# V of twelve blocks loaded as two halves of 64 partitions through two queues, in an attention kernel on one core

## The chip, the cores and the metric

The kernel runs on one core of one Trainium2 chip. The metric is device microseconds of one execution. Before the change the median of 3 runs is 631.32 us (631.2 to 632.54). Durations of single steps come from one profiled execution.

## The reference

Attention without a mask, for 8 x 16 = 128 heads, each with 16 queries, 2048 keys and head size 256, all in bf16:

```
scores = einsum('bhqd,bhkd->bhqk', q, k) * 256 ** -0.5
attn   = softmax(scores, axis=-1)
out    = einsum('bhqk,bhkd->bhqd', attn, v)
```

K and V have 134 MB each and are read once. The output has 1 MB.

## The kernel before, in words

**Blocks.** The 128 heads go in G = 16 blocks of 8 heads (8 heads by 16 queries are the 128 rows of a block's scores). One block needs K in two loads, e = 0 and 1 (below: K0 and K1), each of 128 partitions by T = 64 rows of 256 elements, 4 MiB; and V in one load of 128 partitions by 128 rows, 8 MiB, 64 KB into each partition. The tile `SL` has four slots of one K load each. Slots `VA` and `VB` together, seen as `VW`, hold V; slots `KA` and `KB` hold K0 and K1. There is one buffer for each, so K0 of the next block can come only when the QK matmuls have read the present K0, and V of the next block only when all PV matmuls of the present one are done.

**Queues.** All loads are issued by SyncE (SP), in one queue, in an order written out by hand (`on_sync`, L128). First q, then K of blocks 0 and 1, V of block 0 in two loads, K of block 2, V of block 1 in two loads (one for slot `VA`, one for slot `VB`, each of 128 partitions). Then a loop (L148) with j from 3 to 14: K0 of block j, K1 of block j, and `load_v(j - 1, 0, 2 * T)` (L152), the V load of block j - 1 in one piece: these are the twelve V loads of blocks 2 to 13. Then K of the last block in four loads, and V of blocks 14 and 15 in 3 and 9 pieces along the rows (`PIECES`, L104). Ahead of each load stands a wait for its slot: K for the counter `c_qk` (QK matmuls), V for `c_pv` (PV matmuls; it counts 8 for each block, one for 16 rows, and starts at 8). `load_v(w, 0, 128)` waits for `c_pv >= 8 * w + 8` (L131), and its DMA (L132) adds 16 to `s_v` when it has landed.

**TensorE (PE).** In round r of its loop (L340) it does the QK matmuls of block r (L296, L297), for r up to 13 also 20 spare matmuls into an unused bank (L356), then PV of block r - 1 (L317). Ahead of PV it waits for `c_ev` (the output bank has been evicted), `c_co[0]` (the first half of the weights is in place) and `s_v` (V has landed); in the middle of PV for `s_v0` and `c_co[1]`, the second half's weights.

**VectorE (DVE)** transposes K in place by 4-byte elements (L200: two instructions for K0, two for K1), takes the row maximum (L222), transposes the exponentials (L226, L227) and does part of the copies that set up PV's weights `PTz` (L207, L209).

**ScalarE (ACT)**, in block g (loop at L276): scaled copies of the next queries (L256), the exponential (L282), then `copies(0, (0, 1))` (L269) for the first half of the weights, which wait until PV of the block before is half done; then, for g other than 0, `evac(g + 1)` (L262): it waits for `c_pv >= 8 * (g + 1)`, that is for PV of the block before to end, and evicts its output; then eight copies for the second half. Ahead of its loop ACT adds 1 to each of three counters, `c_ev`, `c_ri` and `c_co[1]` (L271).

**GpSimd (POOL)** makes first increments of 11 semaphores (L168), among them 8 to `c_pv`, then sets buffers to zero and copies q. It has no work after the start.

Of the kernel before, what the change touches and what calls it, by code (L numbers as in the profile page):

```python
# [5 lines left out]
ALU = mybir.AluOpType  # L6
# [8 lines left out]
T = 64  # L15
# [5 lines left out]
def bass_standalone__softmax_full_bidir__sampling_kernel(  # L21
# [11 lines left out]
    last = G - 1  # L33
# [5 lines left out]
    vb = v.rearrange("b h s d -> (b h s) d").rearrange("(g p t) d -> g p t d", p=128, t=2 * T)  # L39
# [3 lines left out]
    with ExitStack() as es:  # L43
# [22 lines left out]
        def sem(name):  # L66
            return ec(nc.semaphore(name))
# [4 lines left out]
        s_kl = [sem("s_kla"), sem("s_klb")]  # L72
        s_v = sem("s_v")
        s_v0 = sem("s_v0")
        s_st = sem("s_st")
        c_pool = sem("c_pool")
        c_qt = sem("c_qt")
# [8 lines left out]
        c_ri = sem("c_ri")  # L86
        c_co = [sem("c_co0"), sem("c_co1")]
        c_mk = sem("c_mk")

        c_pv = sem("c_pv")  # L90
        c_ev = sem("c_ev")
# [16 lines left out]
        VW = SL[:, VA:VB + 1, :, :].rearrange("p a t d -> p (a t) d")  # L108
# [16 lines left out]
        def load_k(eng, g, e, slot, t0, n, s):  # L125
            eng.dma_start(SL[:, slot, t0:t0 + n, :], ku[2 * g + e, :, t0:t0 + n, :]).then_inc(s, 16)  # L126

        def on_sync(eng):  # L128
            def load_v(w, a, n):

                eng.wait_ge(c_pv, 8 * w + (a + n + C - 1) // C)  # L131
                eng.dma_start(VW[:, a:a + n, :], vb[w, :, a:a + n, :]).then_inc(s_p[a] if a else s_v, 16)  # L132

            eng.dma_start(QX, qh).then_inc(s_q, 16)
            for g, s0, s in ((0, VA, s_k0), (1, KA, s_k)):
                for e in range(2):
                    load_k(eng, g, e, s0 + e, 0, T, s[e])

            for e in range(2):
                eng.wait_ge(c_qk, 4 * e + 4)  # L140
                eng.dma_start(VW[:, T * e:T * e + T, :], vb[0, :, T * e:T * e + T, :]).then_inc(s_v0 if e else s_v, 16)
            for e in range(2):
                eng.wait_ge(c_qk, 4 * e + 12)
                load_k(eng, 2, e, KA + e, 0, T, s_k[e])
            for e in range(2):
                eng.wait_ge(c_pv, 4 * e + 12)
                eng.dma_start(VW[:, T * e:T * e + T, :], vb[1, :, T * e:T * e + T, :]).then_inc(s_v0 if e else s_v, 16)
            with nc.Fori(3, last, engines=[SP], hint_back_edge=True) as j:  # L148
                for e in range(2):
                    eng.wait_ge(c_qk, 8 * j + 4 * e - 4)  # L150
                    load_k(eng, j, e, KA + e, 0, T, s_k[e])
                load_v(j - 1, 0, 2 * T)  # L152
            for e in range(2):
                eng.wait_ge(c_qk, 8 * last + 4 * e - 4)
                load_k(eng, last, e, KA + e, 0, T // 2, s_k[e])
                load_k(eng, last, e, KA + e, T // 2, T // 2, s_kl[e])
            for w in PIECES:
                for a, n in PIECES[w]:
                    load_v(w, a, n)
            eng.wait_ge(c_ev, G)  # L160
            eng.dma_start(oh[:, 0:last, :], O_all[:, 2:G + 1, :]).then_inc(s_st, 16)
            eng.wait_ge(c_ev, G + 1)
            eng.dma_start(oh[:, last, :], O_all[:, G + 1, :]).then_inc(s_st, 16)
            eng.wait_ge(s_st, 32)

        def on_gpsimd(eng):

            for x, n in ([(c_pv, 8)] + [(x, 1) for x in s_kl] +  # L168
                         [(s_p[a], 16 * G - 16 * sum(a in dict(PIECES[w]) for w in PIECES)) for a in s_p]):
                eng.sem_inc(x, n)  # L170
            eng.memset(QW[:].rearrange("p e m x -> p (e m x)").bitcast(F32), 0.0).then_inc(c_qt, 1)
            zero = [PTz[:, e].rearrange("p t c -> p (t c)").bitcast(F32) for e in range(2)]
            eng.memset(zero[0], 0.0).then_inc(c_pool, 1)
            eng.memset(mk[:], 1.0).then_inc(c_mk, 1)
            eng.memset(P_sb[:, 0:16], 0.0).then_inc(c_mk, 1)
            eng.memset(P_sb[:, 2064:2080], 0.0).then_inc(c_mk, 1)
            eng.wait_ge(c_mk, 3)
            for r in range(4):
                eng.memset(mk[32 * r:32 * r + 16, :], 0.0).then_inc(c_mk, 1)
            eng.wait_ge(c_qt, 2)  # L180
            for n in range(16):

                eng.wait_ge(c_cq if n else c_pool, max(n, 1))
                eng.tensor_copy(*qx(n // 4, n % 4)).then_inc(c_cq, 1)  # L184

            eng.wait_ge(c_qw, 4)
            eng.wait_ge(c_cq, 16)
            eng.wait_ge(c_mk, 7)
            eng.memset(zero[1], 0.0).then_inc(c_pool, 1)
# [60 lines left out]
        def on_scalar(eng):  # L250
            def qwb(src):
                for a in range(4):
                    dv = QW[32 * a:32 * a + 32, :, 16 * a:16 * a + 64, :]
                    dv = bass.AP(tensor=dv.tensor, offset=QW[32 * a:32 * a + 32, 0, 16 * a, :].offset,
                                 ap=[list(dv.ap[0]), [1024 + 512, 2], [2, 64], [1, 2]])
                    eng.activation(dv, src(a), ACTF.Copy, scale=scale).then_inc(c_qw, 1)  # L256

            def evac(n):

                eng.wait_ge(c_pv, 8 * n)  # L260
                eng.wait_ge(c_ri, n)
                eng.activation(O_all[:, bass.ds(n, 1), :].rearrange("p o d -> p (o d)"), O_ps[:, 0:D], ACTF.Copy,  # L262
                               scale=rinv[:, bass.ds(n, 1)]).then_inc(c_ev, 1)

            def copies(e, rs):
                for r in rs:
                    for x in range(2):
                        dst, src, m = weights(e, r, x)
                        eng.activation(dst, src, ACTF.Copy, scale=m if x else 1.0).then_inc(c_co[e], 1)  # L269

            for x in (c_ev, c_ri, c_co[1]):  # L271
                eng.sem_inc(x, 1)
            eng.wait_ge(c_qt, 2)
            qwb(lambda a: QXu[0:32, a, 0:2, :, :])
            eng.wait_ge(c_pool, 2)
            with nc.Fori(0, G, engines=[ACT]) as g:  # L276
                eng.wait_ge(c_qk, 8 * g + 8)
                qwb(lambda a: QTu[32 * a:32 * a + 32, bass.ds(((g + 1) & 15) * 2, 2), :, :])
                eng.wait_ge(c_mx, g + 1)
                sv = S_ps[:, 0, :]  # L280
                sv = bass.AP(tensor=sv.tensor, offset=sv.offset, ap=[list(sv.ap[0]), [32, 64], [1, 2], [2, 16]])
                eng.activation(P_sb[:, 16:2064], sv, ACTF.Exp,  # L282
                               bias=negm[:], scale=1.0, accum_out=lsum[:]).then_inc(c_ex, 1)
                eng.wait_ge(c_pt, 2 * g + 2)
                eng.wait_ge(c_pv, 8 * g + 4)
                copies(0, (0, 1))
                gg = eng.to_reg(g)
                with eng.If_ne(gg, 0):
                    evac(g + 1)
                copies(1, (0, 1, 2, 3))  # L290

        def on_tensor(eng):
# [35 lines left out]
            with nc.Fori(0, 2, engines=[PE]) as e:  # L328
                for h in range(2):
                    with nc.Fori(0, 4, engines=[PE]) as b:  # L330
# [5 lines left out]
                        if h:  # L336
                            ins.then_inc(c_qk, 1)

            two = eng.alloc_register("two")
            with nc.Fori(1, G + 1, engines=[PE], hint_back_edge=True) as r:  # L340
                rr = eng.to_reg(r)
                r16 = eng.to_reg(16 * r)
                with eng.If_lt(rr, G):
                    for e in range(2):
                        for h in range(2):
                            eng.wait_ge(c_kt[e], 2 * r + h - 1)
                            if e + h == 0:
                                eng.wait_ge(c_ex, rr)
                            ins = qk(e, (2 * h, 2 * h + 1), KA + e)
                        ins.then_inc(c_qk, 4)  # L350

                    mid = eng.to_reg((r + 14) & 15)
                    with eng.If_lt(mid, 13):
                        with nc.Fori(0, SPARE, engines=[PE]) as x:
                            for _ in range(4):
                                mm(X_ps[:], QW[:, 1, :, 7], QT[:, 0:512], True, True, False)  # L356
                eng.wait_ge(c_ev, rr)
                eng.wait_ge(c_co[0], 8 * r)
                eng.wait_ge(s_v, r16)
                eng.reg_alu(two, r16, 32, ALU.min)  # L360
                pv(r16, two)

        on_sync(nc.sync)
        on_gpsimd(nc.gpsimd)
        on_vector(nc.vector)
        on_scalar(nc.scalar)
        on_tensor(nc.tensor)


# [26 lines left out]
```

## Time and profile before

| | |
|---|---|
| median of 3 runs | 631.32 us (631.2 to 632.54) |
| the profiled execution | 631.19 us, of which the span from first to last instruction 629.9 us |
| granted clock of TensorE | 0.978 |
| PE busy | 533.9 us (85%) |
| DVE busy | 419.4 us (67%) |
| ACT busy | 269.0 us (43%) |
| POOL busy | 26.0 us (4%) |
| moved by DMA | 270.54 MB, mean 430 GB/s |

The profile shows one execution. Busy time is an engine's own; instructions that wait or only issue a DMA don't count. The DMA engines have a row of their own. PE's matmuls are pipelined, so 85% busy does not mean that TensorE is at its peak. SPq is SyncE's sequencer, which issues the loads, and lines such as L317 are those of the code above. Where a row ends in brackets, they hold the engine's idle time ahead of it and what ended it.

### The profile page before, as it was taken

Reading aid. Unit: us, or ns where it says so; the run is one execution under the profiler, and the core shown is the slowest. Engines: PE = TensorE matmul, PEld = TensorE weight load, DVE = VectorE, ACT = ScalarE, POOL = GpSimd, SP = SyncE. Lnnn points to the kernel's source line nnn. Section 1 sums busy time; section 2 is a strip of 40 time slices with the busy share of each in tenths; the row PEclk is TensorE's granted clock in tenths of the full one; section 3 lists DMA queues with packets and bytes.
Section 4 is the critical chain, followed back from the end, with each engine's and each line's share of the span. In section 5 each row is a group of like instructions: output and inputs, shape, how many; then the busy total and the mean of one; then the engine's idle time right before and its main releaser. Section 6 shows DMA issues by size and latency. Waiting matters only on the chain.

```text
span 629.9 us, 7712 instructions
## 1 busy us (share of the span) xinstructions
PE 533.9 (85%) x3336; PEld 273.5 (43%) x2561; DVE 419.4 (67%) x193; ACT 269.0 (43%) x308; POOL 26.0 (4%) x30
## 2 busy tenths in 40 slices
PE   1657989889888897888988888988889888889997
PEld 0112734518244272532726336263362724518386
DVE  1989694865849657496574956749466594768740
ACT  1026562823437243362534525335263352732653
POOL 7800000000000000000000000000000000000000
PEclk9998999999898999989989999898999989999999
DMA  9999999999999999999999999999999999999999
GB/s 377 433 433 433 431 429 429 433 433 433 466 400 466 400 433 433 433 433 433 433 466 400 466 400 466 400 433 433 433 433 466 400 466 400 466 400 426 437 420 383
DMA packets 11152, 270.54 MB, mean 430 GB/s; under 512 B 1040, under 2 KB 3344, under 8 KB 3728
## 3 DMA queue, kind: packets, MB, share of 16 engines
q1 hardware_dynamic: 11152, 270.54, 100.0%
HBM read 269.48 MB, written 1.05 MB: 429 GB/s over the span
## 4 chain that ended last, share of the span: by engine, by line
DMA 57%; PE 33%; DVE 5%; issue 5%; SPq 0%; DVEq 0%; ACT 0%
DMA SL<-in_v_dram 51%; PE O_ps L317 31%; DMA SL<-in_k_dram 5%; DVE SL L200 3%; DVE PTb L227 1%; DVE negm L222 1%; PE X_ps L297 1%; PE S_ps L296 1%; PE S_ps L297 1%; DVE PTz L207 0%; DVE PTz L209 0%; SPq L132 0%; SPq L126 0%; ACT P_sb L282 0%; DVE O_all L247 0%
## 5 line engine op out<-in xcount | busy, mean ns | idle before, releaser
L200 DVE STREAM_TRANSPOSE SL<-SL 128x4096 f32<-128x4096 f32 (+1 forms) x63 | 280.6, 4492 | 88.0 <-DMA SL<-in_k_dram 87.6
L296 PE MATMUL S_ps<-SL,QW 128*128 128x512 bf16 (+1 forms) x512 | 205.1, 401 | 59.0 <-DVE SL L200 49.8
L317 PEld LDWEIGHTS O_ps<-SL,PTz 128*128 128x128 bf16 x2048 | 199.0, 98 | 113.9 <-issue 89.0
L317 PE MATMUL O_ps<-SL,PTz 128*128 128x256 bf16 x2048 | 226.4, 273 | 24.8 <-DMA SL<-in_v_dram 23.8
L297 PE MATMUL S_ps<-SL,QW 128*128 128x512 bf16 (+1 forms) x512 | 204.4, 399 | 0.0
L296 PEld LDWEIGHTS S_ps<-SL,QW 128*128 128x128 bf16 (+1 forms) x512 | 74.4, 145 | 230.1 <-issue 160.7
L256 ACT ACTIVATE QW<-QT 32x256 bf16 x64 | 26.8, 419 | 168.4 <-PE S_ps L297 167.2
L269 ACT ACTIVATE PTz<-PTa 16x1024 bf16<-16x1024 bf16 x32 | 33.8, 1056 | 128.9 <-PE O_ps L317 114.2
L222 DVE TENSOR_REDUCE negm<-S_ps 128x1 f32<-128x2048 f32 x16 | 36.6, 2289 | 58.3 <-PE S_ps L297 58.3
L269 ACT ACTIVATE PTz<-PTa,mk 32x1024 bf16<-32x1024 bf16 x64 | 72.3, 1130 | 0.0
L269 ACT ACTIVATE PTz<-PTb 16x1024 bf16<-16x1024 bf16 x64 | 67.2, 1051 | 1.2
L226 DVE STREAM_TRANSPOSE PTa<-P_sb 128x2048 bf16<-128x2048 bf16 x16 | 37.0, 2312 | 35.4 <-ACT P_sb L282 35.4
L297 PE MATMUL X_ps<-QT,QW 128*128 128x512 bf16 x260 | 58.2, 379 | 0.0
L227 DVE STREAM_TRANSPOSE PTb<-P_sb 128x2080 bf16<-128x2080 bf16 x16 | 36.8, 2302 | 0.0
L269 ACT ACTIVATE PTz<-PTb,mk 32x1024 bf16<-32x1024 bf16 x32 | 36.2, 1132 | 0.0
L282 ACT ACTIVATE P_sb<-S_ps,negm 128x2048 bf16<-128x2048 f32 x16 | 31.5, 1967 | 5.9 <-DVE negm L222 5.9
L262 ACT ACTIVATE O_all<-O_ps,rinv 128x256 f32 x15 | 7.1, 473 | 39.8 <-PE O_ps L317 39.8
L184 POOL COPY QT<-PTz 32x1024 bf16<-32x1024 bf16 x16 | 17.4, 1088 | 2.1 <-DVE PTz L194 1.2
L207 DVE TENSOR_SCALAR PTz<-PTb,mk 32x1024 bf16<-32x1024 bf16 x32 | 15.2, 476 | 0.0
L209 DVE COPY PTz<-PTa 16x1024 bf16<-16x1024 bf16 x32 | 13.5, 421 | 1.1
L247 DVE TENSOR_SCALAR O_all<-O_ps,rinv 128x256 bf16<-128x256 f32 x1 | 0.5, 483 | 20.2 <-PE O_ps L317 20.2
L296 PE MATMUL S_ps<-PTz 128*128 128x512 bf16 x1 | 0.6, 609 | 9.7 <-ACT QW L256 9.7
(18 smaller groups left out, 21.0 us busy)
## 6 DMA issues: line engine op xcount, KB each, us to landing
SL<-in_k_dram SPq DMA_DIRECT2D x30, 4096.0 KB, 24.1
SL<-in_v_dram SPq DMA_DIRECT2D x4, 4096.0 KB, 21.3
SL<-in_k_dram SPq DMA_DIRECT2D x4, 2048.0 KB, 22.3
SL<-in_v_dram SPq DMA_DIRECT2D x1, 3840.0 KB, 21.3
SL<-in_v_dram SPq DMA_DIRECT2D x1, 2496.0 KB, 22.0
SL<-in_v_dram SPq DMA_DIRECT2D x1, 2048.0 KB, 12.2
SL<-in_v_dram SPq DMA_DIRECT2D x1, 1856.0 KB, 24.7
SL<-in_v_dram SPq DMA_DIRECT2D x1, 1792.0 KB, 10.8
```

The source lines that it names most:

```text
L184: eng.tensor_copy(*qx(n // 4, n % 4)).then_inc(c_cq, 1)
L200: eng.transpose(x, x).then_inc(c_k0 if first else c_kt[e], n)
L207: ins = eng.tensor_scalar(out=dst, in0=src, scalar1=m, scalar2=None, op0=ALU.mult)
L222: eng.tensor_reduce(out=negm[:], in_=S_ps[:].rearrange("p c n -> p (c n)"), axis=AX.X, op=ALU.max, negate=True).then_inc(c_mx, 1)
L226: eng.transpose(fa[:, 0:2048], P_sb[:, 16:2064]).then_inc(c_pt, 1)
L227: eng.transpose(fb[:, 0:2080], P_sb[:, 0:2080]).then_inc(c_pt, 1)
L256: eng.activation(dv, src(a), ACTF.Copy, scale=scale).then_inc(c_qw, 1)
L269: eng.activation(dst, src, ACTF.Copy, scale=m if x else 1.0).then_inc(c_co[e], 1)
L282: eng.activation(P_sb[:, 16:2064], sv, ACTF.Exp, bias=negm[:], scale=1.0, accum_out=lsum[:]).then_inc(c_ex, 1)
L296: return eng.matmul(dst, w, x, start=start, stop=stop, skip_group_check=not check)
L297: return eng.add_instruction(mybir.InstMatmult(name=nc.get_next_instruction_name(), engine=PE, start_tensor_calc=start, stop_tensor_calc=stop,
L317: ins = eng.matmul(O_ps[:, 0:D], PTz[:, t // T, t % T, :], VW[:, t, :], start=(t == 0), stop=(t == 2 * T - 1))
```

## The change

The V loads of blocks 2 to 13 are each made as two loads of 64 partitions. SP issues the one for partitions 0 to 63 at the old place, with the old wait written out, and it adds 16 to `s_v`. ACT issues the one for partitions 64 to 127, with the same wait, between `copies(0, (0, 1))` and `evac(g + 1)`, for g from 2 to 13; it adds 16 to a new semaphore `s_v1`. PE waits for both ahead of PV: `s_v1` starts at 32, which stands for blocks 0 and 1, and the value waited for stops at 16 * last - 16 = 224, so that blocks 14 and 15 wait for nothing new. The increments of `c_ev`, `c_ri` and `c_co[1]` that ACT made at the start go to GpSimd's list, with the 32 of `s_v1`.

```diff
+        s_v1 = sem("s_v1")
...
 (on_sync, loop over j from 3 to 14)
-                load_v(j - 1, 0, 2 * T)
+                eng.wait_ge(c_pv, 8 * j)
+                eng.dma_start(VW[0:64, :, :], vb[j - 1, 0:64, :, :]).then_inc(s_v, 16)
...
 (on_gpsimd)
-            for x, n in ([(c_pv, 8)] + [(x, 1) for x in s_kl] +
+            for x, n in ([(c_pv, 8), (c_ev, 1), (c_ri, 1), (c_co[1], 1), (s_v1, 32)] + [(x, 1) for x in s_kl] +
...
 (on_scalar)
-            for x in (c_ev, c_ri, c_co[1]):
-                eng.sem_inc(x, 1)
...
                 with eng.If_ne(gg, 0):
+                    mid = eng.to_reg((g + 14) & 15)
+                    with eng.If_lt(mid, last - 3):
+                        eng.wait_ge(c_pv, 8 * g + 8)
+                        eng.dma_start(VW[64:128, :, :], vb[g, 64:128, :, :]).then_inc(s_v1, 16)
                     evac(g + 1)
...
 (on_tensor)
+            one = eng.alloc_register("one")
...
                 eng.wait_ge(s_v, r16)
+                eng.reg_alu(one, r16, 16 * last - 16, ALU.min)
+                eng.wait_ge(s_v1, one)
                 eng.reg_alu(two, r16, 32, ALU.min)
                 pv(r16, two)
```

## The prediction

> **What bounds the kernel now.** I read the page first, then the kernel's middle in one window, then the chain of waits, then single engines in one block. The page's slices of the span, its DMA queues and its chain by engine:
>
> ```profile
> span 629.9 us, 7712 instructions
> ...
> DMA  9999999999999999999999999999999999999999
> GB/s 377 433 433 433 431 429 429 433 433 433 466 400 466 400 433 433 433 433 433 433 466 400 466 400 466 400 433 433 433 433 466 400 466 400 466 400 426 437 420 383
> ...
> q1 hardware_dynamic: 11152, 270.54, 100.0%
> ...
> DMA 57%; PE 33%; DVE 5%; issue 5%; SPq 0%; DVEq 0%; ACT 0%
> ...
> SL<-in_k_dram SPq DMA_DIRECT2D x30, 4096.0 KB, 24.1
> ```
>
> One queue carries everything, its packets fill the sixteen DMA engines for the whole span, and the slices stand at 433 GB/s (466 and 400 alternate around it where a long row falls to one side). The kernel's middle in one window says it again (the last two columns are the DMA engines' share and GB/s):
>
> ```profile
> core 0: us, PE busy (x) PEld busy (x) DVE busy (x) ACT busy (x) POOL busy (x), PEclk, DMA share, GB/s
> 100.00:580.00 480.00, 422.65 (x2668) 215.94 (x2030) 325.52 (x154) 206.91 (x237) 0.00 (x0) 0.98 1.00 432
> ```
>
> At 433 GB/s a K load (4096 KB, 4.19 MB) takes 9.69 us, and V of one block (128 partitions of 64 KB by the code, 8.39 MB) takes 19.37 us. K0, K1 and V of a block together take 38.75 us. The chain of waits, in order of time, through one block:
>
> ```profile
> 233.51 24.23 DMA SL<-in_v_dram
> 257.75 0.23 issue
> 257.98 14.15 PE O_ps L317 x128
> 272.13 0.02 issue
> 272.14 0.04 SPq L132
> ...
> 272.29 24.23 DMA SL<-in_v_dram
> ```
>
> From one V issue to the next are 272.29 - 233.51 = 38.78 us: the bytes' own 38.75. The chain names PE for 14.15 us of it, but these 14.15 us are not idle time of the DMA engines, which move K0 and K1 meanwhile. The loop just closes: V is issued while 24.23 - 19.37 = 4.86 us of the block's second K load (K1) and of start and landing still lie ahead of it in SP's queue. So the time is the bytes over the rate, and an edit counts only if it changes the rate or empties the queue.
>
> **The change, part by part.** (1) *Increments at the start.* The start of the timeline, POOL, ACT and PE:
>
> ```profile
> 1.60 0.95 POOL L171 MEMSET QW<- 128x1024 f32 x1 [1.15 <-issue]
> ...
> 6.19 0.53 POOL L179 MEMSET mk<- 16x1 f32 x4
> 7.91 1.77 ACT L256 ACTIVATE QW<-PTz 32x256 bf16<-32x256 bf16 x4 [5.68 <-DVE PTz L194]
> 7.94 12.51 POOL L184 COPY QT<-PTz 32x1024 bf16<-32x1024 bf16 x11 [1.22 <-DVE PTz L194]
> 9.74 0.61 PE L296 MATMUL S_ps<-PTz 128*128 128x512 bf16 x1 [9.74 <-ACT QW L256]
> ```
>
> POOL's 11 increments of now fit in the 1.15 us ahead of its first big memset, at most 0.1 us each. Four more (the three from ACT and one for the new semaphore) move its memsets by at most 0.42 us. POOL then waits 1.22 us for DVE anyway, and ACT waits for the same transpose, so this costs nothing; without that cover it would be 0.42 us.
>
> (2) *ACT's part in each block.* It issues a DMA ahead of the eviction at L262. SP's own issue from its line, and ACT's timeline around the end of a block:
>
> ```profile
> L132 SPq DMA_DIRECT2D SL<-in_v_dram x24: 327/333/437, 117.4 to 612.4; - x24
> L132 SPq FUSED_REGOPS  x12: 42/43/43, 117.2 to 543.6; - x12
> ...
> 229.47 1.13 ACT L269 ACTIVATE PTz<-PTb,mk 32x1024 bf16<-32x1024 bf16 x1
> 233.51 0.47 ACT L262 ACTIVATE O_all<-O_ps,rinv 128x256 f32 x1 [2.90 <-PE O_ps L317]
> ...
> 241.18 1.13 ACT L269 ACTIVATE PTz<-PTa,mk 32x1024 bf16<-32x1024 bf16 x1
> 252.05 1.75 ACT L256 ACTIVATE QW<-QT 32x256 bf16 x4 [9.74 <-PE S_ps L297]
> ```
>
> The wait that ACT gets (all of PV of the block before) is the one that the eviction has already, and ACT stands idle 2.90 us ahead of it, so ACT's load begins with SP's, near 233.5, and not late. The issue takes about 0.33 us and some register steps of 0.04 us: 0.5 us. Queued behind it on ACT are the eviction and the copies for the second half. They end at 242.8 instead of 242.3, and ACT next works at 252.05; PE needs the evicted bank at 257.98. Cost nothing, 12 x 0.5 = 6 us were it uncovered.
>
> (3) *PE's part.* One register step and one passed wait ahead of PV, by the 0.04 us rows about 0.1 us in each of 15 blocks. They make the next V issue that much later, but up to 4.86 us of transfers are queued ahead of it, so the DMA engines don't notice; 1.5 us if they did.
>
> (4) *V in two halves.* Twelve blocks, 2 to 13. Each half is 64 partitions of 64 KB: 4.19 MB. Every load in this trace spans 128 partitions, so no row shows a load of 64, and I bound it by the two nearest. By bytes a half is a K load: 9.69 us, two of them 19.37, and nothing is lost. By partitions it is the V load with every second row left out: the same 64 KB into each partition, and if a partition can't be filled faster than now (64 KB in 19.37 us; a K load fills 32 KB in 9.69 us, the same 3.4 GB/s), a half takes 19.37 us, as long as the whole. A gain is as good as excluded: the bytes stay, and the rate has stood at 433 with all engines filled, so that the start and the end (377 and 383) are all that lies below it.
>
> I take the upper end. The nearest row is V's own, with the same row length, source and slot, while a K load has other rows. Both rows also leave open that 433 GB/s is a limit of 128 partitions' doors and not of sixteen engines.
>
> Whether the halves overlap decides as much: SP's half stands behind the rest of K1 in its queue, ACT's half does not. ACT's half begins at once beside K1's rest, and SP's follows when that is through. If the sixteen engines serve one piece of a load at a time, and a piece for 64 partitions moves at half rate, the two halves cost 2 x 19.37 = 38.74 us however they are mixed. From a V issue to its landing: 4.86 + 38.74 = 43.60 us, and the period is 43.60 + 0.23 + 14.15 + 0.17 = 58.15 us instead of 38.78, that is +19.37. The bytes' side agrees: 2 x 9.69 + 38.74 = 58.12, so the loop closes as before, with K1's tail in the queue.
>
> What is late next? The upper half can hold K1 back. DVE's, SP's and PE's timelines in the block:
>
> ```profile
> 234.89 13.10 DVE L200 STREAM_TRANSPOSE SL<-SL 128x4096 f32<-128x4096 f32 x3
> ...
> 243.32 8.97 SPq L126 DMA_DIRECT2D SL<-in_k_dram  x2
> ...
> 248.04 0.44 PE L296 MATMUL S_ps<-SL,QW 128*128 128x512 bf16 x1 [0.59 <-DVE SL L200]
> ...
> 251.62 4.48 PE L297 MATMUL X_ps<-QT,QW 128*128 128x512 bf16 x20
> 257.98 2.24 PE L317 MATMUL O_ps<-SL,PTz 128*128 128x256 bf16 x19 [1.88 <-DMA SL<-in_v_dram]
> ```
>
> Two transposes of K1 take 2 x 13.10 / 3 = 8.73 us, the QK matmuls after them 251.62 - 248.04 = 3.58 us, and the spare matmuls 4.48 us: 16.8 us from K1 to PE's being ready for PV. With the whole upper half ahead of it K1 lands 4.86 + 19.37 = 24.2 us after the V issue, and PE is ready at 41.0, ahead of V's 43.6. So this wait stays hidden. The next K0 is issued 9.8 us after V (243.32) and queues behind the lower half in SP's queue; it has waited there before too.
>
> Sum: 12 x 19.37 = 232.4 us. The profiled execution took 631.19 us (span 629.9 and 1.3 around it), 0.13 under the median of the three runs: 631.32 + 232.4 = 863.7. If the seam of the halves overlaps by an eighth, 2.4 us a block are saved: 835. Upward there is the second load's own start and landing, bounded by the smallest transfer of the page:
>
> ```profile
> out_dram<-O_all SPq DMA_DIRECT2D x1, 64.0 KB, 1.8
> ```
>
> Uncovered, 12 x 1.8 = 21.6 us would come on top, with ACT's 6 us of part (2) 891.
>
> [...]
>
> **The rivals.** *Half of it overlaps.* If the two queues share the engines byte by byte and only the partitions' doors limit (216.5 GB/s for each 64), ACT's half spends itself first on K1's rest: 4.86 us of K1 are 2.10 MB, half of them upper; with 2.10 MB of ACT's half the upper door moves 3.15 MB in 14.5 us. Then 2.09 MB of both halves go side by side, 9.7 us, then the lower half's last 2.10 MB alone, 9.7 us: 33.9 us against 24.23, +9.7 in each block, 116 in all: 748 us. For it: one load's start lies beside another's end, and nothing shows the engines unable to mix. Against it: all sixteen are filled by one queue. [...]
>
> *Not slower.* If 433 GB/s is the sixteen engines' limit (27 GB/s each) whatever the partitions, or if both halves run side by side all the time, V's 8.39 MB take 19.37 us as before. For it: the queue row's 100% of sixteen engines at one rate for K and V. What then decides is K1: beside ACT's half its 4.86 us become 9.7, PE is ready 16.8 us later, at 26.5 after the V issue, 2.3 us behind V's 24.23. That delay empties the queue by as much and so shortens K1's tail in the next block (with a tail under 19.37 - 16.8 = 2.6 us nothing is late): from 631 to 631 + 12 x 2.3 = 659 if it never settled, likeliest 631. The point from which it decides is a half that lands in 9.7 us when alone.
>
> *The change doesn't do what it says*: ACT's half would have to start late. ACT's 2.90 us of idle time speak against it, and a start that late would only end the sharing with K1; it has no chance of its own.
>
> **How the numbers follow.** Halves at half rate, one after another: 0.62, with 835 to 890. Partial overlap: 0.18, about 690 to 800. Not slower by the rate: 0.20, of which 0.07 with K1's delay showing (over 632.6), 0.10 unchanged, 0.03 faster by a better filled start and end. About 0.2% (1.3 us) is what a measurement of this kernel can tell from no change. The time is that of the likeliest case, 863; 690 to 890 leaves out the third case. Faster 0.03, same 0.10, slower 0.62 + 0.18 + 0.07 = 0.87.
>
> **What would show it.** Right: the slices in the middle fall from 433 to 16.78 MB / 58.15 us = 289 GB/s while the DMA engines' share stays near full; V's issues stand 58 us apart; the lower half lands some 43 us after its issue and the upper one well before; PE's longest wait for V grows from 1.88 us, K1 lands later, and PE's spare matmuls end ahead of PV. POOL's start and ACT's eviction shift by under 0.5 us. Wrong: slices at 433 throughout (then engines are the limit), about 343 (16.78 MB in 38.78 + 9.7 = 48.5 us: overlap), or PV released by QK and no longer by V.

## The result, and the profile after

The changed kernel takes 878.66 us (median of 6 runs, 876.63 to 880.14) against 631.32 us before: a ratio of 1.3912, 95% interval 1.3896 to 1.3928. It is slower by 247 us, 20.6 us for each of the twelve blocks. The profiled execution took 876.9 us.

The page of the changed kernel, its span, slices, queues and chain by engine:

```profile
span 875.6 us, 7800 instructions
...
PEclk9989998696895986967959959779689597696899
DMA  9999999999999999998989999899999999898999
GB/s 389 433 437 434 433 335 222 335 287 192 431 192 240 383 192 332 290 240 359 263 192 392 231 287 335 192 359 263 214 409 201 278 335 240 311 311 192 386 432 380
...
q1 hardware_dynamic: 10384, 220.21, 72.8%
q10 hardware_dynamic: 960, 50.33, 27.0%
...
DMA 62%; PE 29%; DVE 4%; issue 3%; ACT 1%; DVEq 0%; SPq 0%; ACTq 0%
```

The DMA engines are as full as before, and the same bytes go through the two queues (220.21 + 50.33 = 270.54 MB). But in the middle the slices swing between 431 (nearly all K) and 192 (V), and the mean over the middle is 286 GB/s (last column of the window):

```profile
core 0: us, PE busy (x) PEld busy (x) DVE busy (x) ACT busy (x) POOL busy (x), PEclk, DMA share, GB/s
200.00:780.00 580.00, 341.61 (x2074) 179.05 (x1588) 254.64 (x119) 162.41 (x184) 0.00 (x0) 0.80 1.00 286
```

This is how a slower transfer looks on this page: a full row of engines and a lower row of GB/s. The share of busy engines alone shows nothing here: it is 1.00 in this window at 286 GB/s, and it was 1.00 before at 432 GB/s (100 to 580 us). The second queue, q10, is ACT's: 12 x 4.19 MB. The chain of waits through one block, in order of time:

```profile
357.29 42.22 DMA SL<-in_v_dram
...
399.65 16.15 PE O_ps L321 x128
...
415.83 0.05 ACTq L292
...
415.97 42.51 DMA SL<-in_v_dram
```

The loop is that of before with 42.22 in place of 24.23, and PV with 16.15 in place of 14.15; 415.97 - 357.29 = 58.68 us in place of 38.78. The issues, with the median time to landing in the last column, and PE's waits for V (us in total, times, longest):

```profile
SL<-in_v_dram ACTq DMA_DIRECT2D x12, 42.5
SL<-in_v_dram SPq DMA_DIRECT2D x12, 42.3
```

```profile
PE O_ps L321 <- DMA SL<-in_v_dram: 263.9, 13, 23.0
```

Both halves land together, 42 us after their issue. PE waits up to 23.0 us for V where it was 1.9, and its waits for transposed K have not grown (35.7 us in total, before 49.8 in the same group).

### The profile page after: what moved, and what is told of

Read it like the earlier page. It is cut to its first block, busy times and chain, and to the rows that moved or that the text cites. A ratio compares the mean times of both kernels' runs of the same rounds, so it can differ in the third digit from the quotient of the medians.

```text
span 875.6 us, 7800 instructions
## 1 busy us (share of the span) xinstructions
PE 553.8 (63%) x3336; PEld 285.8 (33%) x2561; DVE 419.6 (48%) x193; ACT 269.2 (31%) x308; POOL 26.1 (3%) x30
## 2 busy tenths in 40 slices
DMA packets 11345, 270.55 MB, mean 309 GB/s; under 512 B 1232, under 2 KB 3536, under 8 KB 3920
## 3 DMA queue, kind: packets, MB, share of 16 engines
q1 hardware_dynamic: 10384, 220.21, 72.8%
q10 hardware_dynamic: 960, 50.33, 27.0%
## 4 chain that ended last, share of the span: by engine, by line
DMA 62%; PE 29%; DVE 4%; issue 3%; ACT 1%; DVEq 0%; SPq 0%; ACTq 0%
DMA SL<-in_v_dram 59%; PE O_ps L321 26%; DMA SL<-in_k_dram 4%; DVE SL L202 2%; PE S_ps L300 1%; PE S_ps L301 1%; ACT PTz L271 1%; DVE PTb L229 1%; DVE negm L224 1%; PE X_ps L301 0%; DVE PTz L209 0%; ACTq L292 0%; DVE PTz L211 0%; SPq L127 0%; ACT P_sb L282 0%
## 5 line engine op out<-in xcount | busy, mean ns | idle before, releaser
L321 PE MATMUL O_ps<-SL,PTz 128*128 128x256 bf16 x2048 | 251.8, 290 | 265.3 <-DMA SL<-in_v_dram 263.9
L321 PEld LDWEIGHTS O_ps<-SL,PTz 128*128 128x128 bf16 x2048 | 211.7, 104 | 366.8 <-issue 329.6
L300 PE MATMUL S_ps<-SL,QW 128*128 128x512 bf16 (+1 forms) x512 | 201.4, 393 | 44.5 <-DVE SL L202 35.7
L301 PE MATMUL S_ps<-SL,QW 128*128 128x512 bf16 (+1 forms) x512 | 200.9, 392 | 0.0
L211 DVE COPY PTz<-PTa 16x1024 bf16<-16x1024 bf16 x32 | 13.5, 421 | 1.1
## 6 DMA issues: line engine op xcount, KB each, us to landing
SL<-in_k_dram SPq DMA_DIRECT2D x30, 4096.0 KB, 44.4
SL<-in_v_dram SPq DMA_DIRECT2D x1, 3840.0 KB, 19.4
```

Source lines behind the costliest of these rows:

```text
L300: return eng.matmul(dst, w, x, start=start, stop=stop, skip_group_check=not check)
L301: return eng.add_instruction(mybir.InstMatmult(name=nc.get_next_instruction_name(), engine=PE, start_tensor_calc=start, stop_tensor_calc=stop,
L321: ins = eng.matmul(O_ps[:, 0:D], PTz[:, t // T, t % T, :], VW[:, t, :], start=(t == 0), stop=(t == 2 * T - 1))
```

## The experiments

The theory at this point: pieces of a load for 64 neighbouring partitions go at half the rate, one half at a time, whatever the queue. The rivals are told with each run. Ratios are to the kernel before.

**One queue.** Is it the second queue?

```diff
 (SP)
+                eng.dma_start(VW[64:128, :, :], vb[j - 1, 64:128, :, :]).then_inc(s_v1, 16)
 (ACT)
-                        eng.dma_start(VW[64:128, :, :], vb[g, 64:128, :, :]).then_inc(s_v1, 16)
...
```

> Both halves of V in SP's queue, the lower ahead of the upper, at the old place; ACT issues none. Theory (pieces for 64 partitions go at half the rate, one half at a time, in whichever queue): two halves of 19.5 to 20 us each follow one another, 870 to 880 us as with two queues. Rival 1 (two queues disturb one another, the engines lose time by turning from one to the other): the loss goes, 631 to 650 us.

Measured: 892.02 us (889.56 to 898.55), 1.4105 (1.4083 to 1.4126). The second queue is not the cause; without it the kernel is 13 us slower still. In one queue the halves come one after the other: the lower lands 24.8 us after its issue and the upper, issued 0.7 us later, 44.4 us after its own, some 20 us between them (medians). SP's issue of the lower half, first and last start, in the changed kernel and then in this one:

```profile
L154 SPq DMA_DIRECT2D SL<-in_v_dram x12: 494/494/561, 117.5 to 770.9; - x12
```

```profile
L154 SPq DMA_DIRECT2D SL<-in_v_dram x12: 494/495/562, 117.4 to 790.2; - x12
```

Eleven periods are 59.40 us each with two queues and 61.16 with one. Less K0 and K1 (19.38) that leaves some 40.0 and 41.8 us for V, which took 19.37. The profiled execution with one queue is the slowest of its five (898.55 us); by the medians, 892.02 and 878.66, the two kernels differ by 1.1 us a block and not by 1.8.

**Two queues, split by rows.** All of the change, but with 128 partitions in each load.

```diff
-                eng.dma_start(VW[0:64, :, :], vb[j - 1, 0:64, :, :])
+                eng.dma_start(VW[:, 0:T, :], vb[j - 1, :, 0:T, :])
-                        eng.dma_start(VW[64:128, :, :], vb[g, 64:128, :, :])
+                        eng.dma_start(VW[:, T:2 * T, :], vb[g, :, T:2 * T, :])
```

> Two queues as in the change, but each load has all 128 partitions and half of the rows (64 of 128). Everything else of the change stays: ACT's issue, the new semaphore, the moved increments. Theory: V takes 19.4 us again, 630 to 634 us. Rival 1 (two queues cost): near 870 us. Rival 3 (ACT's issue ahead of the eviction or the new wait set the period): 635 us or more.

Measured: 632.74 us (632.55 to 633.65), 1.0021 (1.0012 to 1.0030). ACT's issue, PE's wait, GpSimd's increments and the second load together cost about 1.4 us. All the rest lies in how V is cut; the even and odd kernel below keeps the row lengths of the change too.

**Half of the bytes.** Only the lower half is loaded; the upper half of V is left out in blocks 2 to 13.

```diff
-                        eng.dma_start(VW[64:128, :, :], vb[g, 64:128, :, :]).then_inc(s_v1, 16)
...
-                eng.wait_ge(s_v1, one)
```

> For blocks 2 to 13 only the lower 64 partitions of V are loaded, by SP alone; the upper half is left out (stale rows of an earlier block are used) and with it 4.19 MB a block. Theory: half of the bytes take as long as all of them took before, 19.4 to 20 us, so 631 to 640 us. Rival 4 (a half goes at the full rate when it is alone, and only two at once hinder one another): 9.7 us a half, K then sets the DMA's 29 us a block and PE's own work of some 33 us the period, under 600 us.

Measured: 651.29 us (649.6 to 651.92), 1.0304 (1.0288 to 1.0319), more than expected, and slower than the kernel before with 50 MB fewer to load. SP's issues here:

```profile
L154 SPq DMA_DIRECT2D SL<-in_v_dram x12: 494/495/562, 117.4 to 562.5; - x12
```

The period is 445.1 / 11 = 40.46 us, so a half alone takes about 21.1 us, longer than all of V before. Why it takes more than V's 19.37 us is not shown. Rival 4 (only two at once hinder one another) is out.

**Even and odd partitions.** Again two loads of 64, interleaved.

```diff
-                eng.dma_start(VW[0:64, :, :], vb[j - 1, 0:64, :, :])
+                eng.dma_start(VW[0:128:2, :, :], vb[j - 1, 0:128:2, :, :])
-                        eng.dma_start(VW[64:128, :, :], vb[g, 64:128, :, :])
+                        eng.dma_start(VW[1:128:2, :, :], vb[g, 1:128:2, :, :])
```

> Two queues as in the change, but SP loads the even partitions (0, 2, ... 126) and ACT the odd ones. Theory in its first form (what counts is that a load reaches into both halves of the partitions): each load reaches all doors, V takes about 19.4 us, 631 to 640 us. [...] Rival 1 (two queues cost): near 870 us as well, but then the kernel with one queue is fast.

Measured: 632.02 us (631.76 to 633.13), 1.0012 (1.0002 to 1.0021). The page of this kernel, its slices and queues:

```profile
GB/s 368 434 434 432 430 430 432 434 434 432 459 407 457 407 432 441 424 441 428 436 449 416 449 418 447 441 411 453 416 457 416 426 438 426 438 412 431 433 421 364
...
q1 hardware_dynamic: 10384, 220.21, 81.4%
q10 hardware_dynamic: 960, 50.33, 18.4%
```

The same bytes in the same number of packets through the same two queues, and no slice of the middle falls under 400. Both halves of V land 24 us after their issue, as V did before (24.23). That a load has 64 partitions is not what costs; which ones they are is. What one such interleaved load does when it is alone was not run.

**Four quarters.** Was the prediction's reason right, that a partition can't be filled faster than 64 KB in 19.4 us?

```diff
-                eng.dma_start(VW[0:64, :, :], vb[j - 1, 0:64, :, :]).then_inc(s_v, 16)
+                eng.dma_start(VW[0:32, :, :], vb[j - 1, 0:32, :, :]).then_inc(s_v, 16)
+                eng.dma_start(VW[32:64, :, :], vb[j - 1, 32:64, :, :]).then_inc(s_v1, 16)
+                eng.dma_start(VW[64:96, :, :], vb[j - 1, 64:96, :, :]).then_inc(s_v2, 16)
+                eng.dma_start(VW[96:128, :, :], vb[j - 1, 96:128, :, :]).then_inc(s_v3, 16)
...
```

> V of blocks 2 to 13 in four loads of 32 partitions (0 to 31, 32 to 63, 64 to 95, 96 to 127), all in SP's queue. Theory (sixteen engines that write into one half of the partitions at the same moment share 216 GB/s): each quarter has half the bytes of a half and takes half its time, so about the time of the kernel with two halves in one queue, 885 to 905 us. Rival 2 (the prediction's reason: a partition can't be filled faster than 64 KB in 19.4 us): each quarter takes 19.4 us, four of them 77.5, so 631 + 12 x 58 = 1330 us.

Measured: 891.3 us (891.06 to 893.69), 1.4129 (1.4106 to 1.4153), the time of two halves in one queue. The quarters, issued half a microsecond apart, land 13.2, 22.7, 32.4 and 41.9 us after their own issues (medians): one after another, some 10 us each. So a partition gets its 64 KB in about 10 us, twice as fast as the prediction allowed; that reason is out. What the runs show is a limit of partitions taken together, and it is no lower for 32 of them (2.10 MB in some 10 us, about 210 GB/s) than for 64 (4.19 MB in 21.1 us, 199 GB/s).

**Every second partition of one half.** The quarters again, with other members (the destinations in short; the sources go with them).

```diff
-VW[0:32], VW[32:64], VW[64:96], VW[96:128]
+VW[0:64:2], VW[1:64:2], VW[64:128:2], VW[65:128:2]
```

> V of blocks 2 to 13 in four loads of 32 partitions in SP's queue, as in the kernel with quarters (891 us), but each takes every second partition of one half: 0, 2 .. 62; 1, 3 .. 63; 64, 66 .. 126; 65, 67 .. 127. Theory (a load must reach into both halves of the partitions): 880 to 900 us, as the quarters. Rival 6 (what hinders is that neighbouring partitions are written at the same moment): near 632 us.

Measured: 896.1 us (893.06 to 899.84), 1.4195 (1.4146 to 1.4244). Steps of two don't help as long as the load stays in one half of the partitions (the quarters took 891.3 us).

**Source or destination?** The sources of the change with the destinations of the even and odd kernel, and the reverse. Bytes and work are the same, but V lies in the wrong partitions.

```diff
 (spread destination)
+                eng.dma_start(VW[0:128:2, :, :], vb[j - 1, 0:64, :, :])
+                        eng.dma_start(VW[1:128:2, :, :], vb[g, 64:128, :, :])
 (spread source)
+                eng.dma_start(VW[0:64, :, :], vb[j - 1, 0:128:2, :, :])
+                        eng.dma_start(VW[64:128, :, :], vb[g, 1:128:2, :, :])
```

> Two queues and the change's own sources (V rows of partitions 0 to 63 for SP, 64 to 127 for ACT), but SP writes them into the even partitions and ACT into the odd ones. V therefore lies in the wrong partitions for blocks 2 to 13 and their outputs are not the reference's; bytes, row lengths and the work of every engine are the same. Theory (the destination decides): as fast as with even and odd partitions on both sides, 631 to 634 us. Rival 5 (the source decides: sixteen engines that read within 4 MB of memory at the same moment hinder one another): as slow as the change, 870 to 880 us.

> The reverse: SP reads the V rows of the even partitions and writes partitions 0 to 63, ACT reads those of the odd ones and writes 64 to 127. Again V of blocks 2 to 13 lies in the wrong partitions. Theory (destination): 870 to 880 us. Rival 5 (source): 631 to 634 us.

Measured: 632.55 us (631.84 to 633.34), 1.0020 (1.0010 to 1.0030), with the destination spread; 877.48 us (876.86 to 880.8), 1.3915 (1.3885 to 1.3945), with the source spread. The slices of the one and of the other:

```profile
GB/s 383 433 433 430 433 435 433 449 416 433 449 416 449 414 433 447 418 447 418 443 441 412 453 414 451 428 416 445 420 445 441 412 453 412 453 406 428 432 421 376
```

```profile
GB/s 392 437 435 432 432 343 209 335 287 191 413 209 238 384 191 308 314 203 371 239 215 407 239 253 355 206 335 287 191 431 191 263 359 239 311 311 191 387 430 380
```

The destination decides (632.55 against 877.48 us); spreading the rows that are read brings nothing, and taking them in a block costs next to nothing (632.55 us, where the even and odd kernel took 632.02).

**A lag between the engines.** If the loss were only that all sixteen engines are in one half at the same moment, engines that come late to the lower half should help the others. Small loads into a scratch tile, of 8 partitions each, were to make some of the engines late. They add bytes but leave the result alone.

```diff
+                eng.wait_ge(s_x, 128 * j - 256)
+                for a in [0, 1, 2, 3, 32, 33, 34, 35]:
+                    eng.dma_start(SCR[a:a + 32:4, :, :], vb[j - 1, a:a + 32:4, 0:26, :]).then_inc(s_x, 16)
                 eng.wait_ge(c_pv, 8 * j)
                 (both halves in SP's queue)
```

> As the kernel with both halves in SP's queue (892 us), with extra work: ahead of the lower half in each of the twelve blocks SP issues eight small loads of 8 partitions (13 KB each, every fourth of 32 partitions) into a scratch tile that nobody reads. A load of 8 rows can occupy 8 of the 16 engines at most; those 8 come 8 x 0.49 = 3.9 us late to the lower half, by an estimate from 216 GB/s for 8 engines. Theory (the loss is that all sixteen write into the same half at the same moment): the engines that are ahead are in the upper half while the late ones are still in the lower, each microsecond of lag saves two and costs the one, so in spite of more bytes it gets faster, 800 to 850 us. Rival (a load of 64 partitions is slow in itself, whatever the other engines do): the extra work adds up, 892 + 12 x 3.9 = 939 us.

> The same with three small loads in place of eight, a lag of about 1.5 us. Theory: between the kernel with eight and the one with none, 835 to 880 us. Rival: 892 + 12 x 1.5 = 910 us.

Measured: 1054.26 us (1047.75 to 1060.19), 1.6723 (1.6625 to 1.6821), with eight; with three, four runs between 938.12 and 962.11 us. The page with eight counts 12880 packets in SP's queue, where the changed kernel has 10384 + 960 in its two, and 2000 of under 512 B in place of 1232: 16 more for each of the 96 small loads, 8 of them under 512 B. So a small load's data goes in 8 packets, which can occupy 8 of the sixteen engines at most. Both kernels miss the theory and go beyond the rival too: (1054 - 892) / 12 = 13.5 us a block for eight loads of 0.1 MB. The lower half lands 35.9 us after its issue, 11 us later than in the kernel with one queue, and the upper again some 20 us behind it (medians): the loss lies in the small loads and the lower half, and the upper half gains nothing. This speaks against the picture of engines that only stand in one another's way by coming at the same moment; but no trace here shows that an engine did come late. To see whether the small loads' own place in the lower half was to blame, they were spread over both halves:

```diff
-                for a in [0, 1, 2, 3, 32, 33, 34, 35]:
-                    eng.dma_start(SCR[a:a + 32:4, :, :], vb[j - 1, a:a + 32:4, 0:26, :]).then_inc(s_x, 16)
+                for a in range(8):
+                    eng.dma_start(SCR[a:128:16, :, :], vb[j - 1, a:128:16, 0:26, :]).then_inc(s_x, 16)
```

> As the kernel with eight small loads a block (1054 us), but the 8 partitions of each small load lie 16 apart, over both halves, so that they don't write into the same half as the engines that are ahead. Theory in the form in which the lag should help (the loss is only that all sixteen engines are in one half at the same moment): under 892 us in spite of the extra bytes. Rival (a load into one half is as slow for an engine when the other engines are elsewhere): the lag brings nothing and the small loads add up, 892 + 12 x 3.9 = 939 us or more.

Measured: 1110.93 us (1107.45 to 1118.98), 1.7569 (1.7540 to 1.7599): slower again. In a window from 200 to 900 us the engines are no longer full (share 0.90, 225 GB/s).

Why uneven work hurts this much is not settled. That the lag itself does the harm was not tested, since no run made the same small loads without one.

**TensorE's clock.** PV takes 16.15 us instead of 14.15 in the changed kernel, at a granted clock of 0.80. Is that part of the loss?

```diff
-SPARE = 5
+SPARE = 25
```

> The changed kernel with 100 spare matmuls instead of 20 in the rounds up to 13, which fill some 18 us of PE's 22 us wait for V, so that TensorE's granted clock should stay nearer to full and PV near 14.2 us instead of 16 to 17. Theory (the DMA engines are never empty, PV lies beside K0 and K1): no change, 872 to 882 us. Rival 3 (the lower clock is part of the loss): 12 x 2.2 = 26 us less, 850 us.

Measured: 892.6 us (892.2 to 895.2), 1.4152 (1.4129 to 1.4176), outside both expectations. A window in the middle, and SP's issues:

```profile
200.00:780.00 580.00, 498.89 (x2605) 173.97 (x1549) 249.01 (x115) 159.35 (x183) 0.00 (x0) 0.95 1.00 283
```

```profile
L154 SPq DMA_DIRECT2D SL<-in_v_dram x12: 494/495/562, 134.7 to 784.4; - x12
```

The clock is 0.95 instead of 0.80, and the period 649.7 / 11 = 59.06 us, as in the changed kernel (59.40). What is lost is one start: the first V of this kind is issued at 134.7 instead of 117.5, 17.2 us later. Ahead of it, in round 2 (the first of the rounds 2 to 14 that have spare matmuls), PE does these in 21.53 us where they took 4.48, and there it had nothing to wait for. In the periods the clock makes no difference: the DMA engines are full and PV lies beside K. PV itself hardly got shorter, 15.71 and 15.52 us in two blocks of the middle, so the run does not show what a PV of 14.15 us would bring.

## Why the prediction was right

**The direction and the bound** were right: the time is the bytes over the rate, and the rate of V halved (8.39 MB in about 40.0 us, 210 GB/s, where they took 19.37 us at 433). The middle fell to 286 GB/s where 289 was forecast, with the engines' share at 1.00. V's issues stand 59.40 us apart on average (58.68 in the block shown), against 58.15.

**The size.** Two halves were taken as 2 x 19.37 = 38.74 us. They take about 40.0 (59.40 - 19.38), 1.3 us more; 12 x 1.3 = 15 us put the 863.7 to 879, and 878.66 was measured. This is the one term of the sum that was mis-sized: two halves are not simply twice the whole, and a half alone takes even 21.1 us. What the extra time is, no run shows. In rates, the half alone moved its 4.19 MB in 21.1 us at 199 GB/s, and two halves in flight their 8.39 MB in 40.0 us at 210 GB/s, some 5% above that.

**The reason for the upper bound was wrong, and its value right.** The prediction argued from V's row that a partition can't be filled faster than now. The quarters show that it can. By these runs the limit is that of each half of the partitions together: 4.19 MB into one half took some 20 to 21 us, as one load of 64 partitions (21.1 us alone) or as two of 32 (some 10 us each). V's row comes near that (19.37 us): there too each half of the partitions that is written gets 4.19 MB in all. That the bound came out was luck: for quarters the same reason gives 1330 us, and 891.3 was measured.

**Halves one after another, however mixed**: right in the sum (two queues 879, one queue 892), wrong in the order. The upper half was to land long before the lower; they land together, 42.5 and 42.3 us after issue. One reason is visible: at V's issue only 42.2 - 40.0 = 2.2 us of K1 were still queued and not 4.86, since PV had grown by 2.0 us, so there was little of K1 for ACT's half to run beside. This alone does not make them land together; what does, no run shows. K1 was not late either: PE's spare matmuls ended 19.9 us after the V issue and not at 41.0. Why two halves in flight at the same time do not fill both halves of the partitions stays open; the prediction's reason, that the engines serve one piece at a time, was not shown, and the runs with a lag do not bear it out.

**What was costed at nothing** cost about 1.4 us in all, by the kernel that splits by rows. In the changed kernel's timeline of ACT:

```profile
357.29 0.50 ACTq L292 DMA_DIRECT2D SL<-in_v_dram  x1
358.10 0.47 ACT L264 ACTIVATE O_all<-O_ps,rinv 128x256 f32 x1 [3.71 <-PE O_ps L321]
...
373.11 1.76 ACT L258 ACTIVATE QW<-QT 32x256 bf16 x4 [6.21 <-PE S_ps L301]
```

POOL's first big memset moved from 1.60 to 1.92 us, by 0.32 (0.42 was the bound). ACT's issue takes 0.50 us, not 0.33, and moves the eviction by 0.8 us, where under 0.5 was forecast; 6.21 us of idle time behind its copies still hide it.

**The rivals.** No loss (631 us) failed at the point that the prediction named: a half alone takes 21.1 us and not 9.7. Partial overlap (748 us) has a half at half rate too; it failed because the two halves never ran side by side, each at its own rate: 40.0 us for both, where the overlap would have left 33.9 - 4.86 = 29. (Its sign was 16.78 MB in 48.5 us, which are 346 GB/s and not the 343 of the prediction; measured were 286.) No loss was right in one thing, which the even and odd kernel shows: two loads of 64 partitions keep the rate of before between them (432 GB/s from 100 to 580 us, at a share of 1.00), if the partitions of each lie in both halves.

## What to carry to other kernels

Judge a load by the partitions that it writes, not by its bytes or by how many queues it has: where the DMA engines are full, a load that stays within partitions 0 to 63, or within 64 to 127, costs here at least as much as one of twice its bytes over all 128 (21.1 us for 4.19 MB into 0 to 63 alone and some 20 us for 4.19 MB into 64 to 127 behind it in one queue, 19.37 us for 8.39 MB over all). Other ranges, such as 32 to 95, were not run. If a load has to be cut in two, cut it by rows or by even and odd partitions; both kept the full rate (632.7 and 632.0 us). And read the GB/s beside the share of busy DMA engines, since the halved rate of V left the share at 1.00.

## What the runs showed of the hardware that had not been expected

Loads into 32 partitions of one half move their bytes no slower than loads into 64 (891 and 892 us), and steps of two within the half change nothing (896 us). Small loads of 8 partitions ahead of such halves cost 13.5 us a block for 0.85 MB, and more when they are spread over both halves; this stays open. TensorE's granted clock, 0.98 before, fell to 0.80 when PE waited some 22 us in each 59 us, and came back to 0.95 with matmuls that filled the wait.
